# Decay masks of a chunked attention made on chip by scans, and the opening of its queues in another order

## The chip, the cores and the metric

One core of a Trainium2 chip. The time is that of one execution on the device, in microseconds (us); the median of a few runs is compared.

## What is computed

An attention with exponential decay, 2 batches, 8 heads, 768 positions, head dimension 64, whose output goes through two dense layers with a gate each. Cut to what matters:

```python
Dmask = where(rel >= 0, lam[:, None, None] ** rel, 0.0)        # rel = i - j in a block
lam_pow = lam[:, None, None] ** (pos + 1)
for each block b:
    intra = (einsum('bhic,bhjc->bhij', qb, kb) * Dmask) @ vb
    inter = (qb * lam_pow) @ kv_state
    out[block] = intra + inter
    kv_state = lam ** block * kv_state + (kb * lam ** (block - 1 - pos)).T @ vb
x = out as 1536 tokens x 512
x = (h * tanh(softplus(h))) @ w_out,  h = x @ w_in             # 512 -> 2048 -> 512
x = (h * sigmoid(h)) @ w_out2,        h = x @ w_in2
```

The result is held to float32, so the dense layers split each operand into a high and a low part and take three products (high x high, low x high, high x low).

## The kernel before, in words

The kernel works on chunks of 128 positions: 12 chunks, 6 for each batch. A chunk's inputs (k and q by channel, k and v by token) are one tile `xslot` of 128 x 2048; there are four such tiles. Weights come as halves of 128 x 1024 words into four tiles `slot`: (n, 0) is block n of a first layer's weights, (n, 1) of a second layer's. VectorE and ScalarE decode such a half (L97, L98, L125, L129), ScalarE rounds it to its high part `wh` (L169) and POOL makes the low part `wl` (L170). Every load is issued by SP (SyncE), in the order of the program; a load waits for its tile to be free, and those behind it wait with it.

The order of the work is written out by hand: each engine executes its instructions in the order in which the program emits them, and only that order and the waits for data and for free buffers set the times.

For chunk n the functions are these. `emit_S` makes eight matmuls, the scores of eight heads, into two banks, `s` (L292); VectorE multiplies them by the mask `dmask` to `sm` (L294). `emit_kd` multiplies k by the last column of the mask, four heads on ScalarE (L276), four on POOL (L269). `emit_qd` multiplies q by `lamrow` on POOL (L281). `emit_chunk` makes `pc`, the chunk's contribution to the state (eight matmuls, L312), which VectorE adds to the decayed state (L318, L320); then `px`, eight matmuls from the old state (L326) and eight from `sm` (L333); ScalarE and VectorE split `px` into `xh` and `xl` (L340, L341). `emit_decay` multiplies the state by lamrow's last column on POOL (L300). Those 32 small matmuls of a chunk run one behind another on TensorE.

The masks before: lambda is loaded to four rows of `pw`; seven doublings on VectorE (L241) make its powers; they are written to memory as `scr` (L251) and read back twice with a step of one element for each row, so that the row of each partition is shifted by one: that is `dmask` (L255). Eight matmuls with `pick` spread the powers over the partitions (L591), and ScalarE copies them to `lamrow` (L594). `warm` is a run of matmuls on zeros that no result uses.

After the opening, chunks 0 to PH - 1 (PH is 4) run alone. From then on chunk n runs beside step i = n - 4 of the first layer: `emit_h` is the hidden product of 512 tokens with one block of 128 hidden units, twelve matmuls (L390), `activate` its gate, and two steps later `emit_o` the twelve matmuls of the second layer (L417). From step 12 on only the dense layers are left, most of the span.

The two loops, cut (L602 to L656):

```python
for n in range(PH):
    emit_chunk(n, ps_h, "h", lambda: n and emit_S(n + 1, ps_o, "o"))
    ...
for i, (t, f) in enumerate(steps):
    ...
    emit_h(t, f, f == 0)
    if n < N:
        ...
        emit_chunk(n, ps_a, "a", lambda: i < LAG and emit_S(n + 1, ps_o, "o"))
```

Of the kernel before, what the change touches and what calls it, by code (L numbers as in the profile page):

```python
# [7 lines left out]
F32 = mybir.dt.float32  # L8
# [4 lines left out]
ALU = mybir.AluOpType  # L13
# [4 lines left out]
def decay_attention_mish_silu_kernel(  # L18
# [8 lines left out]
    nc = tc.nc  # L27
    P = 128
    N = x.shape[0]
    H = lam.shape[0]  # L30
# [28 lines left out]
    dram = ctx.enter_context(tc.tile_pool(name="dram", bufs=1, space=bass.MemoryType.DRAM))  # L59

# [128 lines left out]
    pw = ac.tile([P, 2, 256], F32, name="pw")  # L189
    nc.vector.memset(pw[:, :, 128:129], 0.0)  # L190
# [16 lines left out]
    R = P // NP  # L207
    nc.sync.dma_start(pw[0:P:R, :, 128:129], lam.rearrange("(p hh o) -> p hh o", hh=2, o=1))
    nc.vector.memset(pw[:, :, 0:127], 0.0)
    nc.vector.memset(pw[:, :, 127:128], 1.0)  # L210
    nc.scalar.preload_act_table_set("mish")
    pick = ac.tile([P, NP, 64], F32, name="pick")
    nc.gpsimd.memset(pick, 0.0)
    for p in range(NP):
        nc.gpsimd.memset(pick[R * p : R * p + 1, p], 1.0)

    nat = {}

    def load_x():
        n = cnt["x"]  # L220
        cnt["x"] += 1
        held["x", n] = xslots.pop(0)
        t = held["x", n].rearrange("p (a c) -> p a c", a=4)
        if n > 1:
            nc.sync.dma_start(t, x[n])
        nat[n] = (
            t[:, 0].rearrange("p (a j) -> p a j", a=NP),
            t[:, 1].rearrange("p (a i) -> p a i", a=NP),
            t[:, 2].rearrange("p (h d) -> p h d", h=H),
            t[:, 3].rearrange("p (h d) -> p h d", h=H),  # L230
        )
        return [lambda i=i: nc.sync.dma_start(t[:, 2 * i : 2 * i + 2], x[n, :, 2 * i : 2 * i + 2]) for i in range(2)]
# [6 lines left out]
    m = 1  # L239
    while m <= 64:  # L240
        nc.vector.tensor_tensor(  # L241
            out=pw[:, :, 128 + m : 128 + 2 * m],
            in0=pw[:, :, 128 : 128 + m],
            in1=pw[:, :, 127 + m : 128 + m].to_broadcast([P, 2, m]),
            op=ALU.mult,
        )
        m *= 2

    dmask = ac.tile([P, 2, NP, C], F32, name="dmask")
    scr = dram.tile([H, 256], F32, name="scr")  # L250
    nc.sync.dma_start(scr.rearrange("(p hh) i -> p hh i", hh=2), pw[0:P:R])  # L251
    x1[0]()
    sap = scr[:, :]
    for hh in range(2):
        nc.sync.dma_start(  # L255
            dmask[:, hh], bass.AP(sap.tensor, sap.offset + hh * 256, [[1, P], [2 * 256, NP], [1, C]])
        )
# [6 lines left out]
    qd, kd, sm = {}, {}, {}  # L264

    def emit_kd(n):
        if n < N and n % CPS < CPS - 1:
            t = kd[n] = at.tile([P, NP, 2, D], F32, tag="kd", name="kd")
            nc.gpsimd.tensor_tensor(  # L269
                out=t[:, 2:], in0=nat[n][2].rearrange("q (p hh) d -> q p hh d", hh=2)[:, 2:],  # L270
                in1=dmask[:, :, 2:, C - 1 : C].rearrange("q hh p o -> q p hh o").to_broadcast([P, 2, 2, D]),
                op=ALU.mult,
            )
            for p in range(2):
                for hh in range(2):
                    nc.scalar.mul(t[:, p, hh], nat[n][2][:, 2 * p + hh], dmask[:, hh, p, C - 1 : C])  # L276
# [6 lines left out]
    def emit_S(n, pool, tag):  # L283
        if n >= N:
            return
        kT, qT, kn, vn = nat[n]
        t = at.tile([P, 2, NP, C], F32, tag="sm", name="sm")
        ss = [pool.tile([P, NP, C], F32, tag=tag, name=f"s{hh}") for hh in range(2)]
        for p in range(NP):
            for hh in range(2):  # L290
                r = slice(64 * hh, 64 * hh + 64)
                nc.tensor.matmul(ss[hh][:, p, :], lhsT=kT[r, p, :], rhs=qT[r, p, :], start=True, stop=True)  # L292
        for hh in range(2):
            nc.vector.tensor_tensor(out=t[:, hh], in0=ss[hh], in1=dmask[:, hh], op=ALU.mult)  # L294
        sm[n] = t
# [9 lines left out]
    def emit_chunk(n, pool, tag, between):  # L305
        c = n % CPS
        vn = nat.pop(n)[3]
        if c < CPS - 1:
            pc = (ps_o if n < PH + LAG else ps_a).tile([P, NP, D], F32, tag="o" if n < PH + LAG else "a", name="pc")
            for p in range(NP):  # L310
                for hh in range(2):
                    nc.tensor.matmul(  # L312
                        pc[64 * hh : 64 * hh + 64, p, :], lhsT=kd[n][:, p, hh, :], rhs=vn[:, 2 * p + hh, :],
                        start=True, stop=True,
                    )
            new = states[(n + 1) % 2]
            if c == 0:
                nc.vector.tensor_copy(new, pc)  # L318
            else:
                nc.vector.tensor_tensor(out=new, in0=pc, in1=new, op=ALU.add)  # L320
        px = pool.tile([P, NP, C], F32, tag=tag, name="px")
        if c > 0:
# [7 lines left out]
        between()  # L330
        for p in range(NP):
            for hh in range(2):
                nc.tensor.matmul(  # L333
                    px[64 * hh : 64 * hh + 64, p, :], lhsT=vn[:, 2 * p + hh, :], rhs=sm[n][:, hh, p, :],
                    start=(c == 0 and p == 0), stop=(p == NP - 1), skip_group_check=True,
                )
# [42 lines left out]
    def emit_h(t, n, first=False):  # L379
# [9 lines left out]
        for wsel, xsel, kk in [(*e, kk) for kk in range(KD) for e in early] + [(*lst, kk) for kk in range(KD)]:  # L389
# [199 lines left out]
    for p in range(NP):  # L589
        for hh in range(2):  # L590
            nc.tensor.matmul(  # L591
                powers[64 * hh : 64 * hh + 64, p, :], lhsT=pick[:, p], rhs=pw[:, hh, 128:256], start=True, stop=True,
            )
    nc.scalar.copy(lamrow, powers)  # L594
    emit_S(0, ps_o, "o")
    warm(6)
    emit_S(1, ps_o, "o")
    warm(4)
    emit_qd(1)
    emit_kd(0)  # L600
    emit_kd(1)
    for n in range(PH):  # L602
# [7 lines left out]
        if n == PH - 1:  # L610
            emit_kd(n + 1)
        pump()
        run_split(2)
# [6 lines left out]
    for i, (t, f) in enumerate(steps):  # L620
# [15 lines left out]
        if n < N:  # L636
            if i < LAG:
                run_parts()
            emit_chunk(n, ps_a, "a", lambda: i < LAG and emit_S(n + 1, ps_o, "o"))
            emit_qd(n + 1)  # L640
# [140 lines left out]
```

## Time and profile before

| | |
|---|---|
| median of 3 runs | 568.9 us (568.27 to 569.68) |
| profiled execution | 568.27 us, span from first to last instruction 566.5 us |
| TensorE (PE) | 559.6 us busy, 99% of the span |
| VectorE (DVE), ScalarE (ACT), POOL | 311.3, 286.6, 163.1 us busy |
| transfers | 50.30 MB, mean 89 GB/s; 16 DMA engines, share by slices of 14 us in the first 43 us: 0.7, 0.9, 0.8 |
| chain that ended last | PE 89%, DVE 3%, DMA 3%, "issue" 2% |

The page gives each engine's busy time, the span in 40 slices, and the chain of waits: from the last instruction back to what released it, or to the instruction before it on its engine. Further views used below are the timeline (instructions in order of time, with the idle time ahead of each and what ended it), the groups of instructions, and the busy time of every engine and of the DMA engines in stretches of 2 us. A matmul of float32 stands in the rows as two records; eight matmuls are sixteen.

### The profile page before, as it was taken

To read this page: it belongs to the slowest core of one execution; us is meant where nothing else is said; L and a number is where in the kernel's file an instruction comes from. 1 tells how busy PE (TensorE), PEld (TensorE's weight loads), DVE (VectorE), ACT (ScalarE), POOL (GpSimd) and SP (SyncE) were. 2 spreads that over 40 slices of the span, in tenths; PEclk is the share of its full clock that TensorE was granted. 3 is DMA by queue.
4 is the path that set the end of the run, shared out by engine and by line. 5 is a ranking of instruction groups with operands and counts; after the bars stand their busy time and mean duration, and the time that the engine had idled before them with its cause. 6 is when DMAs were issued, how large, how long until landed. Compare 5 with 4: busy or idle time off the path is not lost.

```text
span 566.5 us, 7613 instructions
## 1 busy us (share of the span) xinstructions
PE 559.6 (99%) x2963; PEld 456.8 (81%) x2963; DVE 311.3 (55%) x459; ACT 286.6 (51%) x537; POOL 163.1 (29%) x139
## 2 busy tenths in 40 slices
PE   9999999999999999999999999999999999999997
PEld 5777777888887888888888788888888888888886
DVE  3675634684556675535659884334634655455222
ACT  2666441656454573354556874646443653455120
POOL 2564430222215123122263462211312212302000
PEclk9999999999999999999999999999999999999999
DMA  7984710123022132202221141212310221100104
GB/s 234 420 318 156 286 39 1 38 74 113 0 76 75 36 113 75 74 25 87 76 74 38 38 135 51 75 38 74 112 52 24 91 95 55 58 0 1 74 2 148
DMA packets 14216, 50.30 MB, mean 89 GB/s; under 512 B 1504, under 2 KB 2784, under 8 KB 12900
## 3 DMA queue, kind: packets, MB, share of 16 engines
q1 hardware_dynamic: 14180, 49.82, 25.5%
q8 instruction: 23, 0.38, 0.3%
q14 instruction: 13, 0.11, 0.1%
HBM read 46.66 MB, written 3.15 MB: 88 GB/s over the span
## 4 chain that ended last, share of the span: by engine, by line
PE 89%; DVE 3%; DMA 3%; issue 2%; POOL 1%; ACT 1%; SPq 0%; DVEq 0%; POOLq 0%
PE po L417 44%; PE ph L390 18%; PE b L527 10%; PE a L527 6%; PE c L527 3%; PE e L527 3%; DMA xslot<-x 2%; PE px L333 1%; PE s L292 1%; PE px L326 1%; DVE acc L448 1%; PE pc L312 1%; DVE acc L438 1%; POOL qd L281 0%; DVE sl L435 0%
## 5 line engine op out<-in xcount | busy, mean ns | idle before, releaser
L170 POOL TENSOR_TENSOR wl<-dec,wh 128x512 fp32r<-128x512 f32 x64 | 85.2, 1333 | 273.6 <-ACT wh L169 242.7
L417 PE MATMUL po<-gh,wh 128*128 128x512 f32 x192 | 76.0, 396 | 0.1
L417 PE MATMUL po<-gh,wl 128*128 128x512 f32 x192 | 75.0, 391 | 0.1
L417 PE MATMUL po<-wh,gh 128*128 128x512 f32 (+1 forms) x193 | 75.0, 389 | 0.0
L417 PE MATMUL po<-wl,gh 128*128 128x512 f32 (+1 forms) x193 | 75.0, 388 | 0.0
L417 PE MATMUL po<-wh,gl 128*128 128x512 f32 (+1 forms) x193 | 74.9, 388 | 0.0
L377 DVE TENSOR_TENSOR gl<-ph,gh 128x512 fp32r<-128x512 f32 x40 | 27.5, 689 | 72.1 <-ACT ph L376 72.1
L376 ACT ACTIVATE gh<-ph 128x512 fp32r<-128x512 f32 x40 | 23.9, 598 | 81.1 <-PE ph L390 80.9
L390 PE MATMUL ph<-xh,wh 128*128 128x512 f32 x160 | 63.3, 396 | 0.7 <-ACT xh L340 0.7
L390 PE MATMUL ph<-xl,wh 128*128 128x512 f32 x160 | 60.9, 390 | 0.0
L125 DVE SCALAR_TENSOR_TENSOR dec<-dec,slot 128x512 uint32<-128x512 uint32 x64 | 51.0, 797 | 16.9 <-ACT slot L98 16.9
L448 DVE TENSOR_TENSOR acc<-po,acc 128x512 f32<-128x512 f32 (+1 forms) x73 | 45.7, 677 | 23.8 <-PE po L417 23.8
L169 ACT CAST wh<-dec 128x512 fp32r<-128x512 f32 x64 | 39.6, 619 | 37.6 <-DVE dec L129 37.2
L170 POOL TENSOR_TENSOR tl<-t,th 128x512 fp32r<-128x512 f32 x28 | 38.3, 1377 | 65.5 <-ACT th L169 63.9
L417 PE MATMUL po<-gl,wh 128*128 128x512 f32 x192 | 51.4, 390 | 0.0
L129 DVE SCALAR_TENSOR_TENSOR dec<-slot,dec 128x512 uint32<-128x512 uint32 x64 | 49.6, 774 | 1.7
L390 PE MATMUL ph<-xh,wl 128*128 128x512 f32 x160 | 44.4, 390 | 0.0
L417 PEld LDWEIGHTS po<-gh,wh 128*128 128x128 f32 x192 | 36.1, 188 | 9.6 <-DVE acc L448 1.4
L98 ACT ACTIVATE slot<-slot 128x512 uint32<-128x512 uint32 x64 | 42.7, 667 | 0.0
L97 ACT ACTIVATE dec<-slot 128x512 f32<-128x512 f32 x64 | 42.5, 665 | 0.2 <-DMA slot<-w 0.2
L417 PEld LDWEIGHTS po<-wh,gh 128*128 128x128 f32 x193 | 36.3, 188 | 7.8 <-issue 0.3
L417 PEld LDWEIGHTS po<-gh,wl 128*128 128x128 f32 x192 | 36.1, 188 | 7.7 <-POOL wl L170 0.5
(117 smaller groups left out, 950.9 us busy)
## 6 DMA issues: line engine op xcount, KB each, us to landing
slot<-w SPq DMA_DIRECT2D x64, 512.0 KB, 3.6
xslot<-x SPq DMA_DIRECT2D x10, 1024.0 KB, 8.8
out<-acc SPq DMA_DIRECT2D x11, 256.0 KB, 2.1
xslot<-x SPq DMA_DIRECT2D x4, 512.0 KB, 4.3
dmask<-scr SPq DMA_DIRECT2D x2, 256.0 KB, 4.4
out<-acc SPq DMA_DIRECT2D x2, 128.0 KB, 1.9
pw<-lam SPq DMA_DIRECT2D x1, 0.0 KB
scr<-pw SPq DMA_DIRECT2D x1, 8.0 KB
```

The lines of the kernel that those rows point to most:

```text
L97: nc.scalar.activation(decs[n, i].bitcast(F32), high.bitcast(F32), AF.Copy, scale=2.0**-112)
L98: nc.scalar.activation(low, low, AF.Copy, scale=TOP3, bias=2.0**-21 - 0.5)
L125: nc.vector.scalar_tensor_tensor(out=d, in0=d, scalar=3, in1=low, op0=ALU.logical_shift_left, op1=ALU.bitwise_or)
L129: nc.vector.scalar_tensor_tensor(out=d, in0=high, scalar=0x80000000, in1=d, op0=ALU.bitwise_and, op1=ALU.bitwise_or)
L169: nc.scalar.copy(hi, f)
L170: nc.gpsimd.tensor_tensor(out=lo, in0=f, in1=hi.bitcast(F32), op=ALU.subtract)
L376: nc.scalar.activation(to, ps, AF.Mish if mm == 0 else AF.Silu)
L377: later.append(lambda: nc.vector.tensor_tensor(out=gl, in0=ps, in1=gh.bitcast(F32), op=ALU.subtract))
L390: nc.tensor.matmul(ph, lhsT=wi[wsel][:, kk * P : (kk + 1) * P], rhs=xt[xsel][:, kk, :], start=(i == 0), stop=(i == 3 * KD - 1),)
L417: nc.tensor.matmul(po[t][j][:, c], lhsT=lhsT, rhs=rhs, start=(first and wsel + gsel == 0), stop=(last and gsel == 1 and c.stop == T),)
L448: nc.vector.tensor_tensor(out=acc[:, j, c], in0=po[t][j][:, c], in1=acc[:, j, c], op=ALU.add)
L527: nc.tensor.matmul(self.b[dst], lhsT=w[ws][:, kk * P : (kk + 1) * P], rhs=x[xx][:, kk, :], start=(start and i == 0), stop=(i == 5), skip_g ...
```

## The change

The mask is made on the chip. Lambda is loaded into the last eight partitions of a column of zeros, `factors`. POOL makes `unit`, 128 x 128, with ones on its rising diagonal (memset, then affine_select). One matmul of factors, broadcast to 128 columns, with eight columns of unit puts the eight lambdas on every partition (`spread`, copied by ScalarE to `lams`). Eight scans on VectorE, state = lambda x state + unit, give the mask of one head each, the mask's rows shifted by the place of the one. The powers are made from the mask by eight matmuls with `last` (the lambdas on partition 127 alone), now one hh after the other. `emit_chunk` is cut into `emit_state`, `emit_px` and `emit_out`; all loads of chunks are two halves; the opening is emitted in another order. The first hidden product takes its three passes one after the other.

The core of the diff:

```diff
-    pw = ac.tile([P, 2, 256], F32, name="pw")
-    nc.vector.memset(pw[:, :, 128:129], 0.0)
+    factors = ac.tile([P, 1], F32, name="factors")
+    nc.vector.memset(factors, 0.0)
...
-    nc.sync.dma_start(pw[0:P:R, :, 128:129], lam.rearrange("(p hh o) -> p hh o", hh=2, o=1))
+    nc.sync.dma_start(factors[P - H : P], lam)
...
+    unit = ac.tile([P, C], F32, name="unit")
+    nc.gpsimd.memset(unit, 0.0)
+    nc.gpsimd.affine_select(
+        out=unit, in_=unit, pattern=[[1, C]], base=1 - C, channel_multiplier=1, compare_op=ALU.not_equal, fill=1.0
+    )
...
-        if n > 1:
-            nc.sync.dma_start(t, x[n])
...
+        if n < 2:
+            return halves
+        for fn in halves:
+            fn()
...
-    nc.sync.dma_start(scr.rearrange("(p hh) i -> p hh i", hh=2), pw[0:P:R])
     x1[0]()
-    sap = scr[:, :]
-    for hh in range(2):
-        nc.sync.dma_start(
-            dmask[:, hh], bass.AP(sap.tensor, sap.offset + hh * 256, [[1, P], [2 * 256, NP], [1, C]])
-        )
     x1[1]()
...
+        if n == t == 0:
+            order = [(*e, kk) for e in (early[0], lst, early[1]) for kk in range(KD)]
...
-    warm(10)
+    warm(5)
+    spread = ps_a.tile([P, H], F32, tag="a", name="spread")
+    nc.tensor.matmul(
+        spread, lhsT=factors.to_broadcast([P, P]), rhs=unit[:, 0:H], start=True, stop=True
+    )
+    lams = ac.tile([P, H], F32, name="lams")
+    nc.scalar.copy(lams, spread)
+    dmask = ac.tile([P, 2, NP, C], F32, name="dmask")
+    ages = dmask[:, :, :, C - 1]
     lamrow = ac.tile([P, NP, C], F32, name="lamrow")
+    last = ac.tile([P, H], F32, name="last")
+    nc.gpsimd.tensor_tensor(out=last, in0=lams, in1=unit[:, 0:1].to_broadcast([P, H]), op=ALU.mult)
     powers = ps_a.tile([P, NP, C], F32, tag="a", name="powers")
-    for p in range(NP):
-        for hh in range(2):
+    for hh in range(2):
+        for p in range(NP):
+            h = H - 1 - (2 * p + hh)
+            nc.vector.tensor_tensor_scan(
+                out=dmask[:, hh, p], data0=lams[:, h : h + 1].to_broadcast([P, C]), data1=unit, initial=0.0,
+                op0=ALU.mult, op1=ALU.add,
+            )
+    warm(6)
+    emit_S(0, ps_o, "o")
+    for hh in range(2):
+        for p in range(NP):
+            h = H - 1 - (2 * p + hh)
             nc.tensor.matmul(
-                powers[64 * hh : 64 * hh + 64, p, :], lhsT=pick[:, p], rhs=pw[:, hh, 128:256], start=True, stop=True,
+                powers[64 * hh : 64 * hh + 64, p, :], lhsT=last[:, h : h + 1].to_broadcast([P, 64]),
+                rhs=dmask[:, hh, p], start=True, stop=True,
             )
+    emit_kd(0)
     nc.scalar.copy(lamrow, powers)
-    emit_S(0, ps_o, "o")
-    warm(6)
+    emit_qd(1)
+    emit_state(0)
+    emit_px(0)
+    emit_out(0)
+    emit_decay(1)
+    emit_kd(1)
     emit_S(1, ps_o, "o")
-    warm(4)
-    emit_qd(1)
-    emit_kd(0)
-    emit_kd(1)
+    emit_px(1)
+    emit_state(1)
     for n in range(PH):
-        emit_chunk(n, ps_h, "h", lambda: n and emit_S(n + 1, ps_o, "o"))
+        if n > 1:
+            emit_state(n)
+            emit_px(n)
         if n:
+            if n < PH - 1:
+                emit_S(n + 1, ps_o, "o")
+            if n == PH - 2:
+                run_split(2)
+            emit_out(n)
+            if n == PH - 1:
+                emit_S(n + 1, ps_o, "o")
+            if n == PH - 1:
+                emit_kd(n + 1)
             emit_qd(n + 1)
-        emit_decay(n + 1)
+            emit_decay(n + 1)
...
         if n < N:
+            if i == 1:
+                run_parts()
+            emit_state(n)
+            emit_px(n)
             if i < LAG:
+                emit_S(n + 1, ps_o, "o")
+            emit_out(n)
+            emit_qd(n + 1)
+            if not i:
                 run_parts()
-            emit_chunk(n, ps_a, "a", lambda: i < LAG and emit_S(n + 1, ps_o, "o"))
```

Three places of the queues. The first is the opening of VectorE's queue, where the mask is made (pw holds the powers of lambda, s_159 and s_151 are scores of chunk 0). Before:

```order
L209 MEMSET pw 128x2x127
L210 MEMSET pw 128x2
L241 TENSOR_TENSOR pw<-pw 128x2
L241 TENSOR_TENSOR pw<-pw 128x2x2
L241 TENSOR_TENSOR pw<-pw 128x2x4
L241 TENSOR_TENSOR pw<-pw 128x2x8
L241 TENSOR_TENSOR pw<-pw 128x2x16
L241 TENSOR_TENSOR pw<-pw 128x2x32
L241 TENSOR_TENSOR pw<-pw 128x2x64
L294 TENSOR_TENSOR sm<-s_159,dmask 128x512
```

With the change (the scans are printed as SCALAR_TENSOR_TENSOR):

```order
L188 MEMSET factors 128x1
L190 MEMSET zeros 128x32
L594 SCALAR_TENSOR_TENSOR dmask<-lams,unit 128x128 x8
L278 TENSOR_TENSOR sm<-s_151,dmask 128x512
L278 TENSOR_TENSOR sm<-s_152,dmask 128x512
L303 COPY state_99<-pc 128x256
```

The doublings are gone, and the mask itself is written by VectorE; the state of chunk 0 is copied ahead of the masking of chunk 1.

The second is the opening of POOL's queue (qd and kd are the decayed q and k; xslot_102 and xslot_103 hold chunks 0 and 1 before, xslot_100 and xslot_101 now). Before:

```order
L213 MEMSET pick 128x256
L215 MEMSET pick 1x64 x4
L281 ISA
L281 TENSOR_TENSOR qd<-xslot_103,lamrow 128x512
L269 TENSOR_TENSOR kd<-xslot_102,dmask 128x256
L269 TENSOR_TENSOR kd<-xslot_103,dmask 128x256
```

With the change:

```order
L208 MEMSET unit 128x128
L209 ISA
L209 AFFINE_SELECT unit<-unit 128x128
L589 TENSOR_TENSOR last<-lams,unit 128x8
L250 TENSOR_TENSOR kd<-xslot_100,dmask 128x256
L261 TENSOR_TENSOR qd<-xslot_101,lamrow 128x512
```

The instruction printed as ISA stood ahead of POOL's first product and stands ahead of affine_select now, whose output the spread reads.

The third is TensorE between the outputs of chunks 2 and 3 (px<-sm) and the scores of chunk 4. Before:

```order
L333 MATMUL px<-sm,xslot_104 64x128 x8
L312 MATMUL pc<-xslot_105,kd 64x64 x8
L326 MATMUL px<-qd,state_101 64x128 x8
L292 MATMUL s_375<-xslot_102 128x128
L292 MATMUL s_376<-xslot_102 128x128
```

With the change:

```order
L322 MATMUL px<-sm,xslot_102 64x128 x8
L298 MATMUL pc<-xslot_103,kd 64x64 x8
L313 MATMUL px<-qd,state_99 64x128 x8
L322 MATMUL px<-sm,xslot_103 64x128 x8
L271 MATMUL s_378<-xslot_100 128x128
L271 MATMUL s_379<-xslot_100 128x128
```

The output of chunk 3 goes ahead of the scores of chunk 4, and those stand between it and the first hidden product.

## Rows read from the trace of the kernel before

**Rows 1.** The page: span, TensorE's busy time, its granted clock by slices.

```profile
span 566.5 us, 7613 instructions
...
PE 559.6 (99%) x2963; PEld 456.8 (81%) x2963; DVE 311.3 (55%) x459; ACT 286.6 (51%) x537; POOL 163.1 (29%) x139
...
PEclk9999999999999999999999999999999999999999
```

**Rows 2.** The chain of waits, first 80 us: start us, us, engine or transfer.

```profile
0.91 1.89 DMA pw<-lam
...
4.50 2.24 DMA scr<-pw
...
7.74 0.51 SPq L232
...
9.51 10.81 DMA xslot<-x
...
22.89 3.12 issue
...
31.13 1.02 PE px L326 x16
32.15 1.09 PE s L292 x16
33.24 1.02 PE px L333 x16
34.27 2.95 PE ph L390 x12
...
43.30 0.62 PE pc L312 x16
```

**Rows 3.** Timeline, ScalarE's first wait for the mask: start us, us, instruction, idle time before it.

```profile
10.88 0.35 ACT L276 ACTIVATE kd<-xslot,dmask 128x64 f32<-128x64 f32 x1 [3.06 <-DMA dmask<-scr]
```

**Rows 4.** Stretches: busy PE, PEld, DVE, ACT, POOL; granted clock, DMA share, GB/s.

```profile
2.00:4.00 2.00, 2.00 (x7) 0.73 (x6) 0.94 (x6) 0.03 (x1) 0.00 (x0) 1.00 0.52 143
4.00:6.00 2.00, 2.00 (x14) 1.55 (x13) 0.44 (x2) 0.00 (x0) 0.00 (x0) 1.00 0.96 340
...
8.00:10.00 2.00, 2.00 (x18) 1.04 (x16) 0.00 (x0) 0.00 (x0) 1.01 (x1) 1.00 0.98 205
...
14.00:16.00 2.00, 1.88 (x29) 1.43 (x27) 0.69 (x2) 1.50 (x5) 1.20 (x2) 1.00 0.98 410
...
32.00:34.00 2.00, 2.00 (x36) 1.80 (x32) 1.94 (x4) 0.62 (x1) 0.72 (x2) 1.00 0.98 289
```

**Rows 5.** Timeline, ScalarE's decoding of the weight half (0, 1).

```profile
29.23 0.67 ACT L97 ACTIVATE dec<-slot 128x512 f32<-128x512 f32 x1 [0.16 <-DMA slot<-w]
29.81 0.67 ACT L98 ACTIVATE slot<-slot 128x512 uint32<-128x512 uint32 x1
```

**Rows 6.** The page: issues of transfers, KB each, median us to landing.

```profile
slot<-w SPq DMA_DIRECT2D x64, 512.0 KB, 3.6
xslot<-x SPq DMA_DIRECT2D x10, 1024.0 KB, 8.8
```

**Rows 7.** Timeline, TensorE's opening.

```profile
0.99 4.05 PE L203 MATMUL warm<-zeros 128*64 128x512 bf16 x9 [0.99 <-DVE zeros L192]
...
4.85 2.32 PE L591 MATMUL powers<-pw,pick 128*64 128x128 f32 x15
...
7.11 1.16 PE L292 MATMUL s<-xslot 64*128 64x128 f32 x16
```

**Rows 8.** Groups by shape, first 34 us: VectorE's doublings | busy us, mean ns | idle.

```profile
L241 DVE TENSOR_TENSOR pw<-pw 128x128 f32<-128x128 f32 x1 | 0.3, 291 | 0.0
...
L241 DVE TENSOR_TENSOR pw<-pw 128x2 f32<-128x2 f32 x1 | 0.2, 164 | 1.7 <-DMA pw<-lam 1.7
```

**Rows 9.** Timeline, POOL's first memset and its first product.

```profile
0.74 0.31 POOL L213 MEMSET pick<- 128x256 f32 x1 [0.29 <-POOLq L771]
...
8.99 1.26 POOL L281 TENSOR_TENSOR qd<-xslot,lamrow 128x512 f32<-128x512 f32 x1 [7.14 <-DMA xslot<-x]
```

More of the change, by code (lines that the diff above doesn't have):

```diff
@@ L231, in load_x @@
         )
-        return [lambda i=i: nc.sync.dma_start(t[:, 2 * i : 2 * i + 2], x[n, :, 2 * i : 2 * i + 2]) for i in range(2)]
+        halves = [lambda i=i: nc.sync.dma_start(t[:, 2 * i : 2 * i + 2], x[n, :, 2 * i : 2 * i + 2]) for i in range(2)]
+        if n < 2:
+            return halves
+        for fn in halves:
+            fn()
     x0 = load_x()
@@ L281, in emit_qd, with emit_S @@
             nc.gpsimd.tensor_tensor(out=t, in0=nat[n][1], in1=lamrow, op=ALU.mult)
-    def emit_S(n, pool, tag):
+    def emit_S(n, pool, tag, mask=True):
         if n >= N:
@@ L286, in emit_S @@
         kT, qT, kn, vn = nat[n]
-        t = at.tile([P, 2, NP, C], F32, tag="sm", name="sm")
-        ss = [pool.tile([P, NP, C], F32, tag=tag, name=f"s{hh}") for hh in range(2)]
+        ss[n] = [pool.tile([P, NP, C], F32, tag=tag, name=f"s{hh}") for hh in range(2)]
         for p in range(NP):
@@ L291, in emit_S, with emit_mask @@
                 r = slice(64 * hh, 64 * hh + 64)
[L292 to L295, printed above, removed]
+                nc.tensor.matmul(ss[n][hh][:, p, :], lhsT=kT[r, p, :], rhs=qT[r, p, :], start=True, stop=True)
+        if mask:
+            emit_mask(n)
+    def emit_mask(n):
+        t = sm[n] = at.tile([P, 2, NP, C], F32, tag="sm", name="sm")
+        for hh, s in enumerate(ss.pop(n)):
+            nc.vector.tensor_tensor(out=t[:, hh], in0=s, in1=dmask[:, hh], op=ALU.mult)
     def emit_decay(n):
@@ L303, in emit_decay, with emit_state, emit_px @@
             )
-    def emit_chunk(n, pool, tag, between):
+    def emit_state(n):
         c = n % CPS
[L307 to L322, printed above, removed]
+        if c == CPS - 1:
+            return
+        vn = nat[n][3]
+        early = PH <= n < PH + LAG
+        pc = (ps_o if early else ps_a).tile([P, NP, D], F32, tag="o" if early else "a", name="pc")
+        for p in range(NP):
+            for hh in range(2):
+                h = 2 * p + hh
+                nc.tensor.matmul(
+                    pc[64 * hh : 64 * hh + 64, p, :], lhsT=kd[n][:, h, :], rhs=vn[:, h, :], start=True, stop=True
+                )
+        new = states[(n + 1) % 2]
+        if c == 0:
+            nc.vector.tensor_copy(new, pc)
+        else:
+            nc.vector.tensor_tensor(out=new, in0=pc, in1=new, op=ALU.add)
+    def emit_px(n):
+        px = pxs[n] = (ps_h if n < PH else ps_a).tile([P, NP, C], F32, tag="h" if n < PH else "a", name="px")
+        if n % CPS > 0:
             for p in range(NP):
@@ L329, in emit_chunk, with emit_out @@
                     )
-        between()
+    def emit_out(n):
+        px, vn = pxs.pop(n), nat.pop(n)[3]
         for p in range(NP):
@@ L334, in emit_chunk @@
                     px[64 * hh : 64 * hh + 64, p, :], lhsT=vn[:, 2 * p + hh, :], rhs=sm[n][:, hh, p, :],
-                    start=(c == 0 and p == 0), stop=(p == NP - 1), skip_group_check=True,
+                    start=(n % CPS == 0 and p == 0), stop=(p == NP - 1), skip_group_check=True,
                 )
@@ L388, in emit_h @@
         early = [(0, 0), lst[::-1]]
-        for wsel, xsel, kk in [(*e, kk) for kk in range(KD) for e in early] + [(*lst, kk) for kk in range(KD)]:
+        order = [(*e, kk) for kk in range(KD) for e in early] + [(*lst, kk) for kk in range(KD)]
+        if n == t == 0:
+            order = [(*e, kk) for e in (early[0], lst, early[1]) for kk in range(KD)]
+        for wsel, xsel, kk in order:
             nc.tensor.matmul(
@@ L588, in decay_attention_mish_silu_kernel @@
+    nc.gpsimd.tensor_tensor(out=last, in0=lams, in1=unit[:, 0:1].to_broadcast([P, H]), op=ALU.mult)
     powers = ps_a.tile([P, NP, C], F32, tag="a", name="powers")
-    for p in range(NP):
-        for hh in range(2):
+    for hh in range(2):
[4 more added lines that the diff above has]
+                op0=ALU.mult, op1=ALU.add,
+            )
@@ L591, in decay_attention_mish_silu_kernel @@
+    warm(6)
+    emit_S(0, ps_o, "o")
+    for hh in range(2):
+        for p in range(NP):
+            h = H - 1 - (2 * p + hh)
             nc.tensor.matmul(
-                powers[64 * hh : 64 * hh + 64, p, :], lhsT=pick[:, p], rhs=pw[:, hh, 128:256], start=True, stop=True,
+                powers[64 * hh : 64 * hh + 64, p, :], lhsT=last[:, h : h + 1].to_broadcast([P, 64]),
+                rhs=dmask[:, hh, p], start=True, stop=True,
             )
+    emit_kd(0)
     nc.scalar.copy(lamrow, powers)
-    emit_S(0, ps_o, "o")
```

40 lines of the change are left out of this document (11 added, 29 removed).

## The prediction, made before the changed kernel was run

> **What bounds the kernel now.** I read the page first. TensorE is busy for 99% of the span at the full granted clock [rows 1], so only a stretch where it waits, or does work that is no part of the result, can be won. The chain of waits shows where: in the first 31 us it runs through transfers, POOL and "issue"; from 31.13 us its pieces are TensorE's and abut, the hidden product of step 1 (emit_h, chunk 5's round) beginning at 34.27 us [rows 2]. What follows is the same set of matmuls in both kernels, apart from places in the queue that leave every shape and count alone. So the result is the start of that product: what it moves, the end moves.
>
> Two things hold the opening. First the masks. They are written out and read back: the chain has 2.24 us for the small write, and ScalarE's first kd, behind 3.06 us of waiting for the mask, begins at 10.88 us [rows 2, 3]. Until then TensorE has only warm-up, the powers and two scores. Second the stream of loads: from 4 us on the DMA engines are 0.96 to 0.98 busy. While only loads run they move 410 GB/s (14 to 16 us); in 8 to 10 us, with the mask's reads in flight, 205 [rows 4]. The load of chunk 3 is 10.81 us of the chain [rows 2].
>
> Durations come from the profiled execution, 568.27 us with a span of 566.5; the median of three is 568.9, 0.63 higher. I sum against 568.27 and add the 0.63 at the end.
>
> **The change, part by part.**
>
> *Removed: the mask through memory.* Seven doublings, one write and two reads go. The two reads bring 512 KB, and more in lost rate: 8 to 10 us at 205 instead of 410 GB/s is 0.4 MB not moved. At 410 GB/s the two are 2.3 us of stream. SP no longer waits between the loads, so all of chunks 0 to 3 is issued in a row, behind lambda.
>
> *Changed: whole loads of 1024 KB become halves with rows of 4 KB.* Weights have such rows already. The bounds of the rate are 410 GB/s (14 to 16 us, weights and chunks together) and 289 (32 to 34 us, DMA share 0.98) [rows 4]. Count to the load that ScalarE waits for in the old kernel, the weight half it picks up at 29.23 us [rows 5]: six chunks of 1.05 MB and four weight halves of 0.52 [rows 6], 8.4 MB. By 6 us the old stream has moved 2 x 143 + 2 x 340 KB/us, 0.97 MB [rows 4]; the rest takes 18.1 us or 25.7 us, so it lands at 24.1 or 31.7 us. I take 390 GB/s, 25 us, nearer the first: it is the saturated row with loads of both kinds behind one another, while at 32 to 34 us new loads were being issued one by one. Then every load is there before TensorE asks (below).
>
> *Added: the spread.* Lambda lands as before, 1.89 us after its issue, at 2.8 us [rows 2]. Five warm-ups at 0.45 us from 0.99 (nine take 4.05) end at 3.2 [rows 7]. The spread is one 128x8 matmul; no row has it. One of the powers is two records of 0.155 us (fifteen in 2.32) [rows 7]; it lies between that, 0.3, and the 0.6 of two warm-ups with a landing; I take 0.4. Six more warm-ups bring TensorE to 6.3 us. ScalarE's copy of 128x8 costs at most its 128x64 row, 0.35 us [rows 3], so VectorE starts at about 4.0 us.
>
> *Added: eight scans of 128x128.* No row is a scan. VectorE's product takes 0.164 us for 2 elements and 0.291 for 128 [rows 8]: 0.29 each if a scan costs what a product does, 0.42 if each element takes twice as long. Eight are 2.3 or 3.4 us, over at 6.3 or 7.4. Scores of chunk 0 run on TensorE until 8 or so, so neither is on the path; I take 0.35. From about 0.55 each on, they would be.
>
> *Added: the unit matrix.* memset and affine_select on POOL, over before lambda lands at 2.8 us if affine_select costs between POOL's memset of 256 (0.31 us) and its 128x512 product (1.26) [rows 9]. This is the number I know least: an ISA instruction stands just ahead of it. In the old kernel the same ISA stands ahead of the first product, and the row says only that POOL sat idle 7.14 us until 8.99, ended by a load [rows 9]. A first instruction behind the ISA thus costs between nothing and 7 us more. I take nothing, because that idle time was ended by a transfer and not by POOL. The Trainium skill (GPSIMD Engine Reference, section 2.1 Instruction dispatch) speaks against this change: the first call into freshly loaded code pays about 6 us with no instruction to show for it. By that figure the masks would come some 6 us later; no row here shows that POOL's code is fetched anew.
>
> *Moved within the queues.* SP issues ten more loads, at about 0.5 us each [rows 2]; in the saturated stream nobody waits for SP. The first hidden product takes its three passes one after the other, so that the low weights are wanted 2 us later than the high ones; splits and casts shift by a place or two on VectorE, ScalarE and POOL. Work of all three is hidden under TensorE's row of small matmuls; where that cover is gone, the added wait below is its price.
>
> *Moved: powers behind scores of chunk 0; scores of chunk 1 behind output 0; scores of chunk 4 behind output 3.* Ten warm-ups in the old queue after the powers go to none. Powers run by halves of hh, four in a row into the same columns. Sixteen records that alternate take 1.02 us of the chain as px; if nothing overlaps, twice that. I take 1.7.
>
> **The sum.** From the first score to step 1's hidden product TensorE now does, back to back [rows 2]: six scores at 1.09, 6.5; powers, 1.7; five pc at 0.62, 3.1; four px from the state and five from the masks at 1.02, 9.2; the first hidden product, 2.95. That is 23.5 us. The old powers ran at half the speed of the later rows of their form, and the scores at 7.11 us were the first at full speed (1.16 for sixteen) [rows 7], with the granted clock at 1.00 throughout: TensorE works at 1.2 GHz until then and at 2.4 after, some 6 us of unbroken work after its start. Part of score 0 falls before that: 0.6 us more (0.3 if the rise comes at 7.1, 2.8 if only after the powers). For waits I add 0.5 us: pc of chunk 1 needs ScalarE's four kd, which stand behind xh of chunk 0, and has some 0.4 us to spare in my layout; no other wait is nearer.
>
> 6.3 + 23.5 + 0.6 + 0.5 = 30.9 us, against 34.27: 3.4 us earlier. Behind it: chunk 4's load (6.3 MB into the stream) lands near 20 us and is wanted at 23, which is 30.9 less the product, pc, px, two scores and an output; step 1's weights are cast behind the weight half of 25 us, two copies of 0.67 later [rows 5] plus a cast, at 27 us, wanted at 30.9. So the layout holds, and TensorE's own work is the bound. What is late next is nothing for the following rounds: old and new do the same work there, and the old one's pieces abut. 568.3 - 3.4 = 564.9, as a median 565.5 us. Its own range is 564.3 to 567.0: 1.2 better without the wait, with the earlier rise and a shorter spread, 1.5 worse with a rise of the clock that comes late.
>
> **Rivals.**
>
> *POOL's first instruction is late (slower).* If the ISA ahead of affine_select costs L, the unit matrix is there at about 1.5 + L, and the spread with it. Because the spread stands ahead of six warm-ups and of score 0 in TensorE's queue, everything shifts, and not only the masks: with L = 7 score 0 begins at 8.5 + 0.4 + 2.7 = 11.6 us, 5.3 later than in the sum. TensorE also idles from 3.2 to 8.5 us and works the six warm-ups, the scores and the powers at 1.2 GHz, 2 us more than in the sum. 5.3 + 2 - 3.4 is 3.9 us slower than before: 572.8. It decides from about L = 4 on, where the gain is used up. For it: the ISA, and a POOL that did nothing for 7 us. Against it: that stretch ends with a landing, and ScalarE and VectorE waited for transfers as well.
>
> *The stream is the bound anyway.* At the 289 GB/s of 32 to 34 us [rows 4] the weight half lands at 31.7 us; ScalarE stands in line for it, two copies of 0.67 and a cast of about 0.6 behind it release step 1's weights at 33.7, and the product begins there: 0.6 us gained, 568.3. At 340 GB/s (4 to 6 us) it lands at 27.8, and nothing is lost. For it: every load now has short rows, and the DMA share is full. Against it: weights with the same rows went at 410 together with others.
>
> *The small operations are the bound.* Masks early or not, each chunk waits for kd, qd, state and mask in turn. The old chain has 3.12 us of "issue" at 22.89, time in which the chain's engine waited for nothing that the profile shows [rows 2]. If such a wait of 2 us stays in the new order, the gain is 1.5 us: 567.4, no change.
>
> **How the numbers follow.** A measurement of this kernel tells from no change about 0.3%, 1.7 us: faster is below 567.2, slower above 570.6. The forecast has 0.64, nearly all faster; the late POOL 0.15, 0.10 slower and 0.05 within the bound at a smaller L; the slow stream 0.12, half faster and half the same; the small operations 0.09, 0.03 of it faster. Together 0.73 faster, 0.17 the same, 0.10 slower. The range runs from 563.8 (score 0 already at 5.7 us, with no added wait) to 569.0, which takes in the slow stream and the waits and leaves out POOL at its worst, about one in ten, with as much below and between.
>
> **What would show it.** Right: scans begin near 4 us and take 2.3 to 3.4 in all; no ScalarE or VectorE row waits for a mask from a transfer; TensorE has next to no idle from score 0 on; step 1's hidden product begins at 30 to 32 us, and all later pieces have the old distances. Wrong: AFFINE_SELECT ending beyond 5 us; the copy of the spread waiting for it; ScalarE's copies waiting for a weight half beyond 29 us; score 0 or the powers at 1.2 GHz beyond 9 us; or a later piece of the chain that waits for a load where the old one did not.

## The result: 563.6 us, 1.9 us below the forecast

The changed kernel takes 563.56 us (median of four runs, 563.34 to 563.63) against 568.8 of the kernel before in the same comparison, a ratio of 0.9906 (95% interval 0.9888 to 0.9923). The forecast was 565.5 with a range from 563.8: faster, as foretold, but 0.24 us under the low end. The profiled execution took 563.52 us, with a span of 561.7; the page:

```profile
span 561.7 us, 7611 instructions
...
PE 556.1 (99%) x2956; PEld 454.6 (81%) x2956; DVE 312.3 (56%) x458; ACT 286.9 (51%) x538; POOL 164.1 (29%) x137
```

TensorE's busy time fell by 3.5 us and the span by 4.8 [rows 1]: about 1.3 us were idle time, the rest warm-ups and slow rows. The chain of waits, first 80 us (start us, us, engine or transfer):

```profile
5.59 11.96 DMA xslot<-x
...
18.28 1.29 POOL qd L261
19.62 1.09 PE px L313 x16
...
26.38 1.02 PE px L313 x16
27.40 1.09 PE s L271 x16
28.50 1.02 PE px L322 x16
29.52 2.95 PE ph L382 x12
...
38.55 0.62 PE pc L298 x16
```

Step 1's hidden product begins at 29.52 instead of 34.27 us, 4.75 earlier, and the pc that stood at 43.30 is at 38.55, again 4.75 earlier [rows 2]. So the gain is made by 29.5 us and nothing is given back. The masks' write and the 3.12 us of "issue" are gone from the chain; the load of chunk 3 is still in it, now ahead of one POOL product. The timeline up to the pick-up of the weight half (0, 1) by ScalarE (start us, us, instruction, idle time before it):

```profile
1.01 0.29 POOL L209 TENSOR_SCALAR_AFFINE_SELECT unit<-unit 128x128 f32<-128x128 f32 x1
...
3.25 0.60 PE L580 MATMUL spread<-unit,factors 128*128 128x8 f32 x2
...
3.78 2.63 PE L201 MATMUL warm<-zeros 128*64 128x512 bf16 x6
3.89 0.17 ACT L584 COPY lams<-spread 128x8 f32<-128x8 f32 x1 [1.87 <-PE spread L580]
4.16 2.63 DVE L594 TENSOR_TENSOR_SCAN dmask<-lams,unit 128x128 f32<-128x128 f32 x8 [3.23 <-ACT lams L584]
...
6.34 1.16 PE L271 MATMUL s<-xslot 64*128 64x128 f32 x16
...
6.87 0.62 POOL L250 TENSOR_TENSOR kd<-xslot,dmask 128x256 f32<-128x256 f32 x1 [2.29 <-DVE dmask L594]
7.43 1.25 PE L603 MATMUL powers<-dmask,last 128*64 128x128 f32 x13
8.42 0.27 PE L298 MATMUL pc<-xslot,kd 128*64 128x64 f32 x1
...
8.74 0.27 PE L603 MATMUL powers<-dmask,last 128*64 128x128 f32 x1
...
9.13 0.28 PE L322 MATMUL px<-sm,xslot 128*64 128x128 f32 x1
...
19.62 1.09 PE L313 MATMUL px<-qd,state 64*64 64x128 f32 x16 [0.29 <-POOL qd L261]
...
26.53 0.70 ACT L95 ACTIVATE dec<-slot 128x512 f32<-128x512 f32 x1 [2.07 <-DMA slot<-w]
```

The eight scans run from 4.16 to 6.79 us, 0.33 each. Score 0 begins at 6.34, at the full rate of 1.16 us for sixteen records, and the powers follow it at once. From then to 29.5 us the timeline of TensorE names one wait, 0.29 us for qd of chunk 3. Two of the stretches (busy PE, PEld, DVE, ACT, POOL; granted clock, DMA share, GB/s) show the stream:

```profile
8.00:10.00 2.00, 2.00 (x44) 2.00 (x43) 1.25 (x3) 0.59 (x1) 0.29 (x1) 1.00 1.03 350
14.00:16.00 2.00, 2.00 (x44) 1.83 (x42) 1.43 (x3) 0.76 (x2) 0.80 (x2) 1.00 1.00 404
```

In 8 to 10 us it moves 350 GB/s where it moved 205 with the mask's reads in flight (406 in masks_only below, whose loads are whole as before), and the weight half is picked up at 26.53 instead of 29.23 us [rows 4, 5].

### The profile page after: what moved, and what is told of

It is laid out like the page before. It is cut to its first block, busy times and chain, and to the rows that moved or that the text cites. A ratio compares the mean times of both kernels' runs of the same rounds, so it can differ in the third digit from the quotient of the medians.

```text
span 561.7 us, 7611 instructions
## 1 busy us (share of the span) xinstructions
PE 556.1 (99%) x2956; PEld 454.6 (81%) x2956; DVE 312.3 (56%) x458; ACT 286.9 (51%) x538; POOL 164.1 (29%) x137
## 4 chain that ended last, share of the span: by engine, by line
PE 95%; DMA 2%; SPq 1%; DVE 1%; POOL 0%; ACT 0%; issue 0%; DVEq 0%; POOLq 0%
PE po L409 46%; PE ph L382 20%; PE b L519 10%; PE a L519 7%; PE e L519 3%; PE c L519 3%; DMA xslot<-x 2%; PE px L322 2%; PE s L271 2%; PE px L313 1%; PE pc L298 1%; SPq L226 1%; DVE acc L440 1%; POOL wl L168 0%; POOL qd L261 0%
## 5 line engine op out<-in xcount | busy, mean ns | idle before, releaser
L123 DVE SCALAR_TENSOR_TENSOR dec<-dec,slot 128x512 uint32<-128x512 uint32 x64 | 52.5, 820 | 17.4 <-ACT slot L96 16.0
L409 PEld LDWEIGHTS po<-wl,gh 128*128 128x128 f32 x193 | 36.2, 188 | 7.5
```

Source lines behind the costliest of these rows:

```text
L123: nc.vector.scalar_tensor_tensor(out=d, in0=d, scalar=3, in1=low, op0=ALU.logical_shift_left, op1=ALU.bitwise_or)
L409: nc.tensor.matmul(po[t][j][:, c], lhsT=lhsT, rhs=rhs, start=(first and wsel + gsel == 0), stop=(last and gsel == 1 and c.stop == T),)
```

## The experiments

Three theories were on record. A: once the masks are early, TensorE's own queue is the bound. B: the masks' way through memory was the whole cost. C: the new order and the halved loads made the gain. Medians and ratios are to the kernel before in the same comparison; its own median was 568.83 us beside the first four runs, 568.93 beside the next four and 570.27 beside the last three, so small differences between groups are read from spans and from the start of step 1's product in the chain, not from medians.

| run | median us (lowest, highest) | ratio, 95% interval | product at, us |
|---|---|---|---|
| the change | 563.56 (563.34, 563.63) | 0.9906 [0.9888, 0.9923] | 29.52 |
| masks_only | 566.41 (566.12, 566.85) | 0.9957 [0.9942, 0.9972] | 32.35 |
| order_only | 568.52 (566.91, 570.64) | 0.9993 [0.9979, 1.0008] | 34.70 |
| whole_loads | 564.10 (564.02, 564.31) | 0.9916 [0.9900, 0.9933] | 29.96 |
| scans_twice | 565.49 (565.47, 565.51) | 0.9940 [0.9920, 0.9961] | 31.53 |
| late_unit | 569.34 (568.58, 569.71) | 1.0006 [0.9995, 1.0016] | 35.44 |
| no_warm | 564.58 (564.21, 565.04) | 0.9930 [0.9915, 0.9944] | 31.03 |
| order_only_warm | 567.56 (566.99, 569.71) | 0.9984 [0.9973, 0.9995] | 32.92 |
| powers_alternate | 563.88 (563.87, 563.89) | 0.9917 [0.9897, 0.9937] | 29.89 |
| third_early | 563.38 (563.07, 564.02) | 0.9888 [0.9870, 0.9906] | 30.02 |
| both_fixed | 562.50 (562.38, 562.61) | 0.9871 [0.9854, 0.9888] | 28.37 |
| both_fixed_warm4 | 562.92 (562.22, 563.71) | 0.9875 [0.9851, 0.9898] | 29.76 |

### masks_only: the old kernel with the masks made on chip

```diff
-    (pw, its seven doublings, scr, one write and two reads)
+    (factors, unit, spread, lams, eight scans, last; five warm-ups ahead of the spread, five behind)
     (order of chunks, whole loads and the ten warm-ups among the scores: as before)
```

> Before with the masks made on chip, and nothing else: the old order of scores, powers and warm-ups, loads of chunks 2 and on in one piece. Reference spans: before 566.5, with the change 561.7 us; hidden product of step 1 at 34.27 and 29.52 us. Theory A (TensorE's own queue is the bound once the masks are early): the ten warm-ups and the score of chunk 1 that stand ahead of output 0 cost some 2.5 us of TensorE, so hidden product 1 begins near 32 us and the span is near 564.3, 2.2 us gained. Theory B (the trip of the masks through memory was the whole cost, the order is beside the point): 561.7 to 562.3. Theory C (the order and the halved loads gave the gain): 566 or more.

The masks alone bring the product from 34.27 to 32.35 us, 1.9 of the 4.75. The chain of this run:

```profile
4.53 12.78 DMA xslot<-x
...
19.88 4.21 issue
24.13 1.27 POOL wl L169
```

and rows of its TensorE and POOL timelines:

```profile
8.62 1.48 PE L202 MATMUL warm<-zeros 128*64 128x512 bf16 x6
...
24.13 1.27 POOL L169 TENSOR_TENSOR wl<-dec,wh 128x512 fp32r<-128x512 f32 x1 [4.25 <-ACT wh L168]
...
25.00 0.49 PE L369 MATMUL ph<-xh,wh 128*128 128x512 f32 x1 [0.69 <-ACT xh L319]
...
28.17 1.05 PE L291 MATMUL pc<-xslot,kd 128*64 128x64 f32 x16
```

The masks are there at 6.79 us, as in the change, but the old queue still holds ten warm-ups among the first scores (six of them take 1.4 us at 8.62). The scores of chunks 0 and 1 and the output of chunk 0 are done at 13.29 us instead of 11.37, 1.9 later. The rest of the 2.8 us comes around the first hidden product. It follows the output of chunk 3 at once and waits 0.69 us for that output's high part, xh; in the new order the scores of chunk 4 stand between. And POOL, which has waited 4.25 us for ScalarE's wh (the 4.21 of "issue" in the chain), comes late to kd of chunk 4, so that its pc takes 1.05 us instead of 0.69. So theory B falls: earlier masks are worth the full gain only in a queue that has work in that place.

### order_only: the new order and halved loads, masks through memory

```diff
-    (unit, spread, lams, eight scans, last)
+    (pw, its seven doublings, scr, one write and two reads, pick: as in the kernel before)
```

> The changed kernel with the masks and powers made as before (doublings, a write, two reads), the new order and the halved loads kept. Theory A: output 0 waits for the mask, which lands near 11 to 12 us, so score 1 begins near 14 us instead of 10.28 and everything behind it is 3.5 to 4 us later than with the change: span 565.3 to 565.8. Theory B: no gain at all, 566 to 567. Theory C: most of the gain stays, 562 to 563.

No gain: the product is at 34.70. The order without early masks runs dry: TensorE has done scores and powers by 8.55 us, and then its timeline reads

```profile
11.08 0.48 PE L319 MATMUL pc<-xslot,kd 128*64 128x64 f32 x2 [2.52 <-ACT kd L277]
...
14.77 2.08 PE L292 MATMUL s<-xslot 64*128 64x128 f32 x16
...
18.62 1.16 PE L292 MATMUL s<-xslot 64*128 64x128 f32 x16
```

The same sixteen records take 2.08 us at 14.77 and 1.16 at 18.62. The stretches show why (granted clock is the third number from the end):

```profile
8.00:10.00 2.00, 0.55 (x12) 0.31 (x6) 0.00 (x0) 0.00 (x0) 0.00 (x0) 1.00 0.87 235
...
12.00:14.00 2.00, 2.00 (x26) 2.00 (x27) 0.54 (x2) 0.65 (x2) 1.39 (x3) 0.50 0.89 254
```

After TensorE stood idle for 2.5 us the granted clock is 0.50, that is 1.2 GHz, until some time in 16 to 18 us. The wait costs twice: 2.7 us of lateness (pc at 11.08 against 8.42 in the changed kernel) and then the slow rows. Theory C falls with this run, and the expectation from A was wrong as well, because it left the clock out.

### order_only_warm: the same, with TensorE kept at work

```diff
                 lhsT=pick[:, p], rhs=pw[:, hh, 128:256], start=True, stop=True,
             )
+    warm(10)
     emit_kd(0)
```

> The run with the new order and the masks through memory, with ten warm-ups behind the powers, so that TensorE works through the 2.5 us in which it waited for the mask (8.55 to 11.08 us). Theory (half the missing gain of the order was lost to the clock, which fell after that wait): the ten warm-ups end at 11 us, pc, px and scores from there run at full speed, product of step 1 at 32.8 us instead of 34.70, span 565.0, median 566.6. Rival (the slow rows there have another cause, or the loads set the end anyway): rows stay at half speed or the time is lost again at chunk 3, product at 34 to 34.7 us, median 568 to 568.5.

```profile
7.73 2.32 PE L202 MATMUL warm<-zeros 128*64 128x512 bf16 x10
11.31 0.33 PE L319 MATMUL pc<-xslot,kd 128*64 128x64 f32 x2 [1.26 <-ACT kd L277]
...
13.84 1.16 PE L292 MATMUL s<-xslot 64*128 64x128 f32 x16
```

In the profiled execution (the fastest of ten) pc comes no earlier (11.31): at the full rate the ten warm-ups end at 10.05 instead of 11, and 1.26 us of the wait are left. But every row after it is at the full rate, and the product is at 32.92 instead of 34.70: between these two executions 1.8 us were the clock's. The median fell by only 1.0 us, and the ten runs reach from 566.99 to 569.71; that the clock still falls in some of them after the 1.26 us is likely (two show a mean granted clock of 0.996) but their rows were not seen. What is left against the change, 3.4 us, is pc starting 2.9 later and its own waits for kd, the lateness of the masks.

### whole_loads: chunks 2 and later in one transfer of 1024 KB

```diff
-        for fn in halves:
-            fn()
+        nc.sync.dma_start(t, x[n])
```

> The changed kernel with the loads of chunks 2 and on in one piece again. If 4 KB rows cost rate (the lower of the two rates of the prediction), the stream is faster and the span falls by 0.5 us or more below 561.7. If halves only let the score begin before the second half is there, score 3 (at 16.61 us) waits for the whole of chunk 3, which lands near 17.5 us, and the span rises by 0.3 to 1.0 us. If neither matters, 561.7 within 0.2.

```profile
17.47 1.16 PE L270 MATMUL s<-xslot 64*128 64x128 f32 x16 [1.48 <-DMA xslot<-x]
```

Score 3 needs only keys and queries, the first half of chunk 3, and now waits 1.48 us for the whole. TensorE's rows reached the full rate earlier in this execution (score 0 at 5.65), and that lead is lost in the wait: the product comes 0.44 us later than in the change, and the median is 0.54 higher. The halves are worth half a microsecond.

### scans_twice: each scan done twice

```diff
+            for _ in range(2):
                 nc.vector.tensor_tensor_scan(
```

> Each scan is made twice, so VectorE ends the mask near 9.4 us instead of 6.8. If the masks are still on the path, output 0 moves from 9.1 to about 10.8 us and the span rises by 1.2 to 1.6 us, to 563.1 or so. If they have slack, as the prediction said of scans below 0.55 us each, it rises by less than 0.3.

```profile
4.16 6.31 DVE L595 TENSOR_TENSOR_SCAN dmask<-lams,unit 128x128 f32<-128x128 f32 x16 [3.23 <-ACT lams L584]
...
10.55 0.62 POOL L250 TENSOR_TENSOR kd<-xslot,dmask 128x256 f32<-128x256 f32 x1 [5.97 <-DVE dmask L595]
```

The masks are there 3.7 us later (10.47 against 6.79) and the product comes 2.0 later, more than expected. Score 1 is 2.44 us later (12.72 against 10.28), so 1.2 us were covered there, and 0.4 more is won back later, at the wait for qd among others. Beyond that the scans are on the path: powers, POOL's kd and with them pc wait for the last one. At 0.33 us each they cost nothing; the point from which they would is (2.63 + 1.2) / 8 = 0.48 us each, near the 0.55 of the prediction.

### late_unit: the price of the late POOL

```diff
+    idle = ac.tile([P, 1024], F32, name="idle")
+    for _ in range(7):
+        nc.gpsimd.memset(idle, 0.0)
     unit = ac.tile([P, C], F32, name="unit")
```

> The changed kernel with seven POOL memsets of 128x1024 (about 0.95 us each) ahead of the unit matrix, so that it is there at about 8 us instead of 1.3: the price of a late POOL, which the prediction put at 5.3 us of shift and 2 us of slow clock. Theory A (TensorE's queue is the bound, the spread stands ahead of six warm-ups and score 0): spread at 8.0, score 0 at 11.2 instead of 6.34, step 1's hidden product 4.9 us later, and up to 2.4 us more for score 0 and powers at half speed after the idle stretch: product at 34.4 to 36.9 us, span 566.6 to 569.0. Rival (what TensorE loses in the queue it gains back later, because loads or small operations were the real limit): product at 31 to 32 us, span 563 to 564.

```profile
8.29 0.59 PE L583 MATMUL spread<-unit,factors 128*128 128x8 f32 x2 [4.97 <-POOL unit L212]
...
11.52 2.08 PE L274 MATMUL s<-xslot 64*128 64x128 f32 x16
13.53 1.50 PE L606 MATMUL powers<-dmask,last 128*64 128x128 f32 x13
```

The spread comes 5.04 us later, score 0 and part of the powers run at half rate, pc of chunk 0 comes 6.3 later (14.76 against 8.42), and the product 5.92 later, at 35.44. Theory A stands: of what TensorE loses in the opening it wins back only 0.4 us. The median returns to that of the kernel before. The prediction's rival of the late POOL had the right mechanism and a price somewhat too high (5.3 + 2 us foretold, 5.0 + 1.3 at pc), but its condition did not come: in the changed kernel affine_select begins at 1.01 us and takes 0.29. The Trainium skill (GPSIMD Engine Reference, section 2.1, Instruction dispatch) gives some 6 us for the first call into freshly loaded code. No such time stands ahead of affine_select here; whether its code was loaded before the first row, no run shows.

### no_warm: one warm-up instead of eleven

```diff
-    warm(5)
+    warm(1)
...
-    warm(6)
```

> The changed kernel with one warm-up ahead of the spread instead of five and none behind it instead of six. Score 0 can then begin when the first half of chunk 0 lands, at about 5.5 us instead of 6.34. Theory A with a clock that depends on the work before: score 0, powers, pc and px of chunk 0 run at half speed (scores 2.1 to 2.3 us, powers 2.4), 2 to 4 us lost against 0.8 won: product of step 1 at 31 to 33 us, span 563 to 565. Rival (the warm-ups only fill time): product at 28.7 us, span 560.9.

```profile
5.25 2.08 PE L271 MATMUL s<-xslot 64*128 64x128 f32 x16 [2.19 <-DMA xslot<-x]
7.26 2.24 PE L602 MATMUL powers<-dmask,last 128*64 128x128 f32 x13
...
12.18 1.16 PE L271 MATMUL s<-xslot 64*128 64x128 f32 x16
```

Score 0 begins 1.1 us earlier, as soon as its half has landed, but score 0, the powers, pc and most of px run at half rate until some 11 us, and the product comes 1.5 us later than in the change. The warm-ups pay for themselves. The granted clock is shown as 1.00 throughout this opening; only the rows' durations tell that TensorE is at 1.2 GHz.

### powers_alternate, third_early, both_fixed: what is left

powers_alternate puts hh inside p in the loop of the powers, so that records alternate between the two halves of the columns:

```diff
-    for hh in range(2):
-        for p in range(NP):
+    for p in range(NP):
+        for hh in range(2):
```

> The changed kernel with the powers issued hh inside p, so that records alternate between the two column halves. Theory (two matmuls in different column halves overlap, in the same half they don't): powers take 1.1 us instead of 1.5, and everything from pc of chunk 0 on comes 0.3 to 0.4 us earlier, product of step 1 at 29.1 to 29.2 us, span 561.3, unless qd of chunk 3 (a wait of 0.29 us now) holds it, then 561.6. Rival (powers already overlap with pc behind them): no more than 0.1 us.

```profile
7.27 1.09 PE L603 MATMUL powers<-dmask,last 128*64 128x128 f32 x16
...
16.78 1.16 PE L271 MATMUL s<-xslot 64*128 64x128 f32 x16 [0.65 <-DMA xslot<-x]
```

From the powers to the first px it takes 1.39 us (7.27 to 8.66) instead of 1.70 (7.43 to 9.13), the 0.3 expected, and score 2 starts at 12.46 instead of 13.01 (0.16 of that because score 0 began earlier). Then score 3 waits 0.65 us for chunk 3, and the product is at 29.89, later than in the change. The load takes back more than was won; it also came later than in the change, whose score 3 began at 16.61 without a wait. So theory A holds in the changed kernel only up to the stream, which is next to it. third_early therefore moves the load, and POOL's qd of chunk 3 ahead of its kd:

```diff
     load_x()
-    load_w(0, 0)
-    load_x()
+    x3 = load_x()
+    x3[0]()
+    load_w(0, 0)
+    x3[1]()
     load_w(1, 0)
```

> The changed kernel with the first half of chunk 3 (keys and queries, 512 KB) issued ahead of the first weight half, and qd of chunk 3 ahead of kd of chunk 3 in POOL's queue, so that neither waits for the second half of chunk 3. Theory (in the changed kernel chunk 3's load holds only its own qd, 0.29 us; all else is TensorE's queue): product of step 1 at 29.2 us instead of 29.5, span 561.4, median 563.3. Rival (the stream of loads is the bound): the weight half that now lands 1.3 us later releases the first hidden product late, product of step 1 at 30 us or more, span 562.3.

```profile
19.24 0.94 PE L300 MATMUL pc<-xslot,kd 128*64 128x64 f32 x16
```

The wait for qd is gone, and the chain up to step 1's product is TensorE's alone. But most of the 0.29 us is spent again: pc of chunk 3 takes 0.94 us here, where that of chunk 2 takes 0.63 (its kd still need the second half of the chunk, which ScalarE and POOL pick up at 18.5). And in this execution score 0 took 1.63 us, since its rows reached the full rate only within it. The product is at 30.02; from the end of score 0 on it comes 0.1 us sooner than in the change. The median is 563.38. The gain of 0.3 us did not come. both_fixed has both edits, and px of chunk 3 ahead of its pc:

> The run third_early with the powers alternating between the two column halves (0.4 to 0.5 us shorter on TensorE), and px of chunk 3 ahead of its pc. Theory (the alternating powers brought no gain by themselves because score 3 then waited 0.65 us for chunk 3's first half): product of step 1 at 28.6 to 28.8 us, span 560.8 to 561.0, median 562.7. Rival (the weight half (0,1), picked up by ScalarE at 26.53 us, is the next bound and lands later still): product at 29.3 us or later, span 561.5 or more.

```profile
15.67 10.86 DMA slot<-w
26.56 0.67 ACT dec L95
27.23 0.58 ACT slot L96
27.81 0.51 ACT wh L167
...
28.37 3.03 PE ph L384 x12
```

562.50 us, all four runs below all those of the change, although the kernel before was slower in this comparison (570.27). The product begins at 28.37, 1.15 us earlier. The chain now runs through the weight half: TensorE waits 0.34 us for its cast. Here theory A ends; the load of step 1's weights is the bound. But 0.91 of the 1.15 us are there before score 0, which begins at 5.43 in this execution because the six warm-ups ahead of it take 1.72 us instead of 2.63. How much of the gain is the edits' is not separated: only one of the four executions has rows.

> The run both_fixed with four warm-ups behind the spread instead of six. Theory (score 0 can begin when chunk 0's first half is there, at 5.5 us, and the clock has risen by then): score 0 at 5.6 to 5.9 us, product of step 1 at 28.3 us, where the weight half of step 1 becomes the bound, span 560.5, median 562.3. Rival (the two warm-ups bought the rise of the clock): score 0 at half speed, 0.5 to 1 us lost, span 561 to 561.5.

```profile
5.63 2.08 PE L273 MATMUL s<-xslot 64*128 64x128 f32 x16
7.64 1.97 PE L605 MATMUL powers<-dmask,last 128*64 128x128 f32 x16
```

Four warm-ups instead of six give two groups of runs: 562.22 and 562.25, 563.60 and 563.71. The profiled one, of the second group, has scores and powers at half rate. With six warm-ups all four runs lay within 0.23 us; that the two more prevent the slow opening is what these eight runs suggest.

## Why the prediction was right in kind and wrong in size

*The place and the bound: right.* The gain is what step 1's product moves (4.75 us, span 4.8), later pieces keep their distances, and TensorE's own work is the bound (late_unit: 5.0 us of delay at the spread, 5.9 at the product).

*Start of score 0 at 6.3 us: right* (6.34), with the spread to 3.8 and six warm-ups of 0.43. *Scans at 0.35: right* (0.33). *affine_select at nothing: right*, so the rival of the late POOL did not come.

*The work of 23.5 us: 0.6 too long.* This is the step of the sum that failed, and the failing term is the powers, 1.7 us with a whole pc of 0.62 behind them. By themselves the powers take 1.58 us (7.43 to 9.01), near the 1.7. But I forgot that pc, which begins in the other half of the columns, overlaps with the last of them, from 8.42 on: powers and pc of chunk 0 take 1.70 us together instead of 2.32. Up to score 1, 0.5 of the 0.6 us lies here.

*The clock, 0.6 us: nothing in the profiled execution.* I expected the rise inside score 0, at 7.1 us or later. It came before 6.34. This was not an error of mechanism: third_early, with the same instructions up to the powers, has score 0 at 1.63 us. It was a choice of one value for something that differs from one execution to the next.

*Waits of 0.5 us: 0.29,* and not for kd of chunk 1 but for qd of chunk 3.

Together: 24.6 us foretold from score 0 to the product, 23.2 measured; the three terms, 0.6 + 0.6 + 0.2, are the 1.4 us by which the profiled execution (563.52) lies below the sum of 564.9. With the 0.63 for the median, of which 0.04 came, they make up the 1.9 us.

*The 0.63 us of the median: wrong.* I took the distance between profiled run and median of the old kernel over to the new one, whose median is 0.04 above its profiled run. The distance belongs to the old opening: beside the experiments it was run 39 times, and the nine executions with a mean granted clock of 0.996 or 0.997 took 569.68 to 570.95 us, the thirty with 0.999 or more 568.23 to 569.79. The four runs of the changed kernel stay within 0.3 us. That the old kernel's waits for the masks are what lets its clock fall is argued from order_only, not shown: no such execution of it was looked at.

*The range's low end, 563.8,* let score 0 come early (0.6 us) and the wait go (0.5). These two lead from 565.5 to 564.4 only; 563.8 comes out if the 0.63 is left off, or the clock's 0.6 taken off too, and the prediction does not say which. The powers it held as certain, so the 0.6 us that went there lies outside it. *The stream at 390 GB/s:* the half was picked up at 26.53 us instead of the 25 worked out. Its cast is ready at 28.3, 1.2 us ahead of the product, so the term held, with less to spare than I thought; powers_alternate and both_fixed show that this is the next bound. *The slow stream and the small operations* did not decide here, though the second is what masks_only shows in the old order. The prediction took the 3.12 us of "issue" for time in which the engine waited for nothing that the profile shows. The timeline of the kernel before names it: POOL's wl at 26.05 us stands behind 3.16 us of waiting for ScalarE's wh, as behind 4.25 in masks_only.

## What to carry to other kernels

Parts of a change need not add up: the masks alone gained 2.4 us of the median, the order alone 0.3, both together 5.2, because early operands need a queue that has work for them, and a queue without filler needs operands that come early. Price a wait of TensorE with what follows it: 2.5 us of idle time also cost 1.8 us of slow rows in order_only. And before a part is shortened, look which load is next: 0.3 us won in the powers was lost at chunk 3 until the load was moved as well.

## What was not expected of the hardware

The time at which TensorE's rows reach the full rate differs between executions with the same instructions up to there: score 0 begins at the full rate at 5.43 us (both_fixed), 5.65 (whole_loads), 6.18 (powers_alternate) and 6.34 (the change), and is at it only in part from 6.48 on (third_early, 1.63 us). The Trainium skill (TensorE: Matmul & The Clock Gate, section "What's actually happening") says that the length of the slow beginning differs from run to run and that it should not be fitted to a fixed count; these runs agree. In both_fixed_warm4 the two groups of runs lie 1.4 us apart; rows were seen of one run, in the slower group.

The granted clock in the profile shows the fall after an idle time (0.50 in order_only from 12 us) but reads 1.00 in an opening in which the rows run at half rate (no_warm, 5 to 11 us). Matmuls that alternate between the two halves of the columns took 1.09 us for sixteen, those with four in a row in one half about 1.6. And a transfer that the masks no longer make gives more than its bytes: 205 to 235 GB/s in 8 to 10 us with the mask's reads in flight, 350 in the changed kernel and 406 in masks_only without. masks_only loads the chunks as the kernel before does, so the halves are not the cause.
